# A fused spectral filter and feed-forward kernel: the column transforms halved by parity, the inverse in four PSUM banks, and part of LN2 moved into the first feed-forward block

## The chip, the cores and the metric

The kernel runs on one core of a Trainium2 chip. The metric is device time in microseconds (us). A profile's "span" runs from the first to the last instruction and is about 1.9 us shorter than the time. Each run also has a state; here "fast" runs have a granted TensorE clock of 0.99 or more. The engine names in the profile are PE (TensorE, matmul), PEld (its weight loads, which overlap matmuls), DVE (VectorE), ACT (ScalarE), POOL (GpSimd) and SP (SyncE, which issues DMAs). Matmuls write their results into PSUM banks; an "eviction" is the copy of such a result into SBUF, where the other operands lie. LN1 and LN2 are the two layer normalisations.

## The reference, cut to what matters

```python
x = A_x                                              # 1 x 2048 x 576, bf16
h = x + _A_ref(_layernorm(x), A_w_r, A_w_i)          # A: rfft2, times a complex filter, irfft2
h2 = h + _B_ref(_layernorm(h), w_gate, w_up, w_down) # B: (gelu(x @ w_gate) * (x @ w_up)) @ w_down, inner width 4608
```

The 2-D Fourier transform runs over 2048 positions and 576 channels (289 frequencies in the channel direction). The kernel does it with matmuls against tables of cosines and sines.

## The kernel before

The kernel has four stages, and inside the second and third each engine works through a fixed order of instructions.

1. **Start**: x is loaded, LN1 statistics are taken, and the position transform is begun.
2. **Filter loop**, 16 groups of frequencies. Per group: D (channel transform, matmuls), B (mixing, matmuls), an eviction Y, the complex product with the filter (T1, T2, then Z), and V (first step back, matmuls, then an eviction into SBUF). Within a turn of the loop the order is D of group i, B of group i-1, V of group i-3.
3. **Inverse**, 16 tiles: I (back to channels), an eviction G, N (back to positions), the residual add on VectorE, and the sum of squares for LN2. Four tiles are also normalised and transposed on TensorE for the first feed-forward block.
4. **FFN**: four blocks of gate and up matmuls (70 us) and down matmuls (35 us).

```python
    def st_D(i):                       # 2 x 5 matmuls of 289 columns
        ...
        for o in range(2):
            b = 2 * sl + o
            for dt in range(5):
                P.op(PE, ... t.matmul(bank(b, 0, 128, 0, K2), U[:, dt, g, :, :], FT[:, dt, o, 0:K2], start=(dt == 0), stop=(dt == 4)), ...)
            # o == 0: VectorE copies the bank to CUS; o == 1: ScalarE does

    def st_B(i):                       # 4 matmuls of 289 columns into banks 4 and 5, ScalarE evicts both to YS
        ...
        P.op(DVE, ... T1 = YS * WS ...)                              # 580 columns
        for pl in range(2):
            P.op(DVE, ... T2[pl] = YS[pl] * WS[1 - pl] ...)          # 290 columns each
        P.op(DVE, ... ZS[0] = T1[0] - T1[1] ...)
        P.op(DVE, ... ZS[1] = T2[0] + T2[1] ...)

    def st_V(i):                       # 4 matmuls of 256 columns to bank 6, 4 of 128 (half the array) to bank 7
        ...
        P.op(ACT, ... V[0:4] <- bank(6) ...)                         # 512 columns
        P.op(DVE, ... V[4] <- bank(7) ...)                           # 128 columns

    for i in range(NG + 3):
        if i < NG:
            st_D(i)
        if 1 <= i <= NG:
            st_B(i - 1)
        if i >= 3:
            st_V(i - 3)

    def st_I(c): ...                   # 2 x 5 matmuls of 288 columns, ScalarE evicts to GS
    def st_N(c): ...                   # 2 matmuls of 288 columns, VectorE adds to x (sum kept), ScalarE squares (sum kept)
```

(The cuts are marked with dots; comments are added.)

Of the kernel before, what the change touches and what calls it, by code (L numbers as in the profile page):

```python
# [11 lines left out]
ZW = 320  # L12
# [17 lines left out]
def build_tables():  # L30
# [28 lines left out]
    T["ITAB"] = I.reshape(128, 16 * 128)  # L59

    d = np.arange(D)[:, None]
    k2 = np.arange(K2)[None, :]
    ph = 2 * np.pi * ((d * k2) % D) / D
    fd = np.zeros((640, 2, KW))
    fd[:D, 0, :K2] = np.cos(ph)
    fd[:D, 1, :K2] = np.sin(ph)
    fd[:, 0, 0] = 0.0
    T["FTAB"] = fd.reshape(5, 128, 2 * KW).transpose(1, 0, 2).reshape(128, -1)

    B = np.zeros((2, 3, 16, 4, 2, 128))  # L70
# [40 lines left out]
    T["BTAB"] = B.reshape(2, 3, 128, 128).transpose(2, 0, 1, 3).reshape(128, -1)  # L111
# [3 lines left out]
    dc = np.arange(D)[None, :]  # L115
# [6 lines left out]
    dt_ = np.zeros((5, 128, D))  # L122
    dt_[0], dt_[1] = C[0:128], N[0:128]
    dt_[2], dt_[3] = C[128:256], N[128:256]
    dt_[4, 0:33] = C[256:289]
    dt_[4, 64:96] = N[256:288]
    T["EYE"] = np.eye(128)
    T["DTAB"] = dt_.transpose(1, 0, 2).reshape(128, -1)
# [156 lines left out]
def _build(nc, A_x, A_w_r, A_w_i, B_w_gate, B_w_up, B_w_down, out):  # L285
# [34 lines left out]
    FT = sb.alloc("FT", [128, 5, 2, KW], BF16)  # L320
    BT = sb.alloc("BT", [128, 2, 3, 128], BF16)
# [12 lines left out]
    V = sb.alloc("V", [128, 5, NT, NG, 8], BF16)  # L334
    DT = sb.alloc("DT", [128, 5, D], BF16)
    IT = sb.alloc("IT", [128, NT, 128], BF16)
    GS = sb.alloc("GS", [128, 2, D], BF16)
# [22 lines left out]
    P.op(POOL, lambda g: g.memset(WS[:, :, :, K2:KW], 0.0), w=["Wz"])  # L360
    P.op(POOL, lambda g: g.memset(U[64:128, 4, :, :, :], 0.0), w=["Uz"])
    xv = A_x[0].rearrange("(p c) d -> p c d", c=NT)
    ov = out[0].rearrange("(p c) d -> p c d", c=NT)
    for i, (c0, c1) in enumerate(((0, 2), (2, 4), (4, 8), (8, 12), (12, 16))):
        P.dma(SP, XO[:, c0:c1, :], xv[:, c0:c1, :], f"x{i}", w=[("X", c) for c in range(c0, c1)])
# [5 lines left out]
    def w_loads(pl, hf, eng):  # L371
        g0, g1 = ((1, 9), (9, 16))[hf]
        src = (A_w_r, A_w_i)[pl]
        o = []
        for jj in range(4):
            o.append((WS[jj:64:4, g0:g1, pl, 0:K2], (16 * jj + g0) * K2, [[128 * K2, 16], [K2, g1 - g0], [1, K2]], jj))
            o.append((WS[64 + jj:128:4, g0:g1, pl, 0:K2], (64 + 16 * jj + 16 - g0) * K2, [[128 * K2, 16], [-K2, g1 - g0], [1, K2]], 4 + jj))
        if hf:
            for p0 in range(2):
                o.append((WS[64 * p0:64 * p0 + 64, 0, pl, 0:K2], 64 * p0 * K2, [[128 * K2, 16], [16 * K2, 4], [1, K2]], 8 + p0))  # L380
        return [lambda d=d, off=off, ap=ap, h=h: P.dma(eng, d, bass.AP(src.tensor, off, ap), f"w{pl}{hf}", r=["Wz"], w=[("W", hf, pl, h)]) for d, off, ap, h in o]

    for f in w_loads(0, 0, SP) + w_loads(0, 1, SP):
        f()
# [3 lines left out]
    P.dma(SP, IT[:, :, :].rearrange("p a b -> p (a b)"), dram["ITAB"][:, :], "it", w=["IT"])  # L388
    P.dma(SP, IDT[:, :], dram["EYE"][:, :], "eye", w=["IDT"])

    P.op(POOL, lambda g: g.memset(YS[:, :, :, K2:KW], 0.0), w=["Yz"])
    P.op(POOL, lambda g: g.memset(ZS[:, :, :, K2:ZW], 0.0), w=["Zz"])
    for f in w_loads(1, 0, POOL):
        f()
    wrest = w_loads(1, 1, POOL)


    def ln1_act(q):
        c = 4 * q + 3
        P.op(ACT, lambda a, c=c: a.activation(JNK[:, 0, :], XO[:, c, :], ACTF.Identity, accum_out=SA[:, 0, c:c + 1]),  # L400
             r=[("X", c)], w=[("SA0", c), "J0"])
        P.op(ACT, lambda a, c=c: a.activation(JNK[:, 1, :], XO[:, c, :], ACTF.Square, accum_out=SA[:, 1, c:c + 1]),  # L402
             r=[("X", c)], w=[("SA1", c), "J1"])
# [5 lines left out]
    def ln1_var(q):  # L409
        for c in range(4 * q, 4 * q + 3):  # L410
            P.op(DVE, lambda v, c=c: v.bn_aggr(MV1[:, c, :], ST1[:, c, :, :]), r=[("ST1", c, 0), ("ST1", c, 1)], w=[("MV1", c)])
        c = 4 * q + 3
        P.op(DVE, lambda v, c=c: v.scalar_tensor_tensor(TM[:, 0, c:c + 1], SA[:, 0, c:c + 1], 1.0 / (D * D), SA[:, 0, c:c + 1],
                                                        op0=ALU.mult, op1=ALU.mult), r=[("SA0", c)], w=[("TM", c)])
        P.op(DVE, lambda v, c=c: v.scalar_tensor_tensor(MV1[:, c, 1:2], SA[:, 1, c:c + 1], 1.0 / D, TM[:, 0, c:c + 1],
                                                        op0=ALU.mult, op1=ALU.subtract), r=[("SA1", c), ("TM", c)], w=[("MV1", c)])

    def ln1_sqrt(q):
        cs = slice(4 * q, 4 * q + 4)
        P.op(ACT, lambda a, cs=cs: a.activation(RS1[:, cs], MV1[:, cs, 1], ACTF.Sqrt, bias=EPT[:, 0:1]),  # L420
             r=[("MV1", c) for c in range(4 * q, 4 * q + 4)] + ["EPT"], w=[("SD1", q)])

    def ln1_scale(q, eng):
        cs = slice(4 * q, 4 * q + 4)
        P.op(DVE, lambda v, cs=cs: v.reciprocal(RS1[:, cs], RS1[:, cs]), r=[("SD1", q)], w=[("RS1", q)])
        if eng == POOL:
            P.op(POOL, lambda g, cs=cs: g.tensor_tensor(ATS[:, cs, :], ATB[:, cs, :], RS1[:, cs].unsqueeze(2).to_broadcast([128, 4, 128]), op=ALU.mult),
                 r=[("RS1", q), "ATB"], w=[("ATS", c) for c in range(4 * q, 4 * q + 4)])
        else:
            for c in range(4 * q, 4 * q + 4):  # L430
                P.op(DVE, lambda v, c=c: v.tensor_scalar(ATS[:, c, :], ATB[:, c, :], RS1[:, c:c + 1], None, op0=ALU.mult),
                     r=[("RS1", q), "ATB"], w=[("ATS", c)])
# [5 lines left out]
    def a_mm(q, dt):  # L438
        b = (5 * q + dt) % 7
        w = 128 if dt < 4 else 64  # L440
        for i in range(4):
            c = 4 * q + i
            P.op(PE, lambda t, b=b, w=w, i=i, c=c, dt=dt: t.matmul(bank(b, 0, w, 128 * i, 128 * i + 128), XO[:, c, 128 * dt:128 * dt + w],
                                                                  ATS[:, c, :], start=True, stop=True),
                 r=[("X", c), ("ATS", c)], w=[("PS", b)])

    def a_ev(q, dt, eng):
        b = (5 * q + dt) % 7
        w = 128 if dt < 4 else 64
        src = bank(b, 0, w).rearrange("p (n g e) -> p n g e", n=4, g=16)  # L450
        dst = U[0:w, dt, :, 4 * q:4 * q + 4, :].rearrange("p g n e -> p n g e")
        if eng == DVE:
            P.op(DVE, lambda v, s=src, d=dst: v.tensor_copy(d, s), r=[("PS", b)], w=[("U", q, dt)])
        else:
            P.op(ACT, lambda a, s=src, d=dst: a.activation(d, s, ACTF.Copy), r=[("PS", b)], w=[("U", q, dt)])  # L455

    P.op(ACT, lambda a: a.activation(SA[:, 0, 0:1], EPT[:, 0:1], ACTF.Sqrt), r=["EPT"], w=[("SA0", 0)])
    ln1_act(0)
    ln1_act(1)
    idle_mm(24)  # L460
    for c in range(3):
        ln1_tile(c)
    ln1_var(0)
    ln1_sqrt(0)
    ln1_act(2)
    ln1_tile(4)
    ln1_scale(0, POOL)
    for f in wrest[:4]:
        f()
    ln1_tile(5)  # L470
    ln1_tile(6)
    ln1_var(1)
    a_mm(0, 0)
    a_ev(0, 0, ACT)
    ln1_sqrt(1)
    for dt in range(1, 5):
        a_mm(0, dt)
    a_ev(0, 1, ACT)
    a_ev(0, 2, ACT)
    ln1_tile(8)  # L480
    ln1_scale(1, POOL)
    for f in wrest[4:7]:
        f()
    ln1_tile(9)
    ln1_tile(10)
    ln1_var(2)
    a_ev(0, 3, ACT)
    a_ev(0, 4, ACT)
    ln1_sqrt(2)
    ln1_act(3)  # L490
    idle_mm(4)
    for dt in range(5):
        a_mm(1, dt)
        a_ev(1, dt, ACT)
    ln1_tile(12)
    ln1_scale(2, POOL)
    for f in wrest[7:]:
        f()
    ln1_tile(13)
    ln1_tile(14)  # L500
    ln1_var(3)
    ln1_sqrt(3)
    idle_mm(4)
    for dt in range(5):
        a_mm(2, dt)
    a_ev(2, 0, ACT)
    a_ev(2, 1, DVE)
    ln1_scale(3, DVE)
    a_ev(2, 2, ACT)
    a_ev(2, 3, DVE)  # L510
    a_ev(2, 4, ACT)
    idle_mm(4)
    for dt in range(5):
        a_mm(3, dt)
        a_ev(3, dt, (ACT, DVE)[dt % 2])
    idle_mm(3)


    ukeys = [("U", q, dt) for q in range(4) for dt in range(5)] + ["Uz"]

    def st_D(i):
        g = GORD[i]
        sl = i % 2
        for o in range(2):
            b = 2 * sl + o
            for dt in range(5):
                P.op(PE, lambda t, b=b, o=o, dt=dt, g=g: t.matmul(bank(b, 0, 128, 0, K2), U[:, dt, g, :, :], FT[:, dt, o, 0:K2],  # L527
                                                                 start=(dt == 0), stop=(dt == 4)),
                     r=ukeys + ["FT"], w=[("PS", b)])
            if o == 0:  # L530
                P.op(DVE, lambda v, b=b, sl=sl: v.tensor_copy(CUS[:, sl, 0, 0:K2], bank(b, 0, 128, 0, K2)), r=[("PS", b)], w=[("CU", sl)])
            else:
                P.op(ACT, lambda a, b=b, sl=sl: a.activation(CUS[:, sl, 1, 0:K2], bank(b, 0, 128, 0, K2), ACTF.Copy), r=[("PS", b)], w=[("SU", sl)])  # L533

    def st_B(i):
# [3 lines left out]
        for b, tabs in ((4, (0, 1)), (5, (1, 2))):  # L539
            for o in range(2):  # L540
# [238 lines left out]
```

## Time and profile before

The time before is 518.28 us (median of 4 runs; 518.22 to 519.13). TensorE is busy for almost the whole span; the first lines of the profile's page are:

```profile
span 516.4 us, 10131 instructions
## 1 busy us (share of the span) xinstructions
PE 507.4 (98%) x4425; PEld 295.9 (57%) x4427; DVE 184.5 (36%) x428; ACT 152.7 (30%) x285; POOL 27.8 (5%) x48
```

The chain of waits, in order of time, has these columns: start (us), duration (us), engine and what it did. This is one full turn of the filter loop and one tile of the inverse, in the kernel before:

```profile
29.36 1.34 PE PS L527 x10
30.70 0.50 PE PS L541 x4
31.20 0.44 PE PS L560 x4
31.64 0.24 PE PS L564 x4
31.87 1.34 PE PS L527 x10
...
67.02 1.23 PE PS L602 x10
68.25 0.24 PE PS L611 x2
68.49 1.23 PE PS L602 x10
```

L527 is D, L541 is B, L560 and L564 are V, L602 is I and L611 is N. Everything on the chain is TensorE, so the loop has a period of 31.87 - 29.36 = 2.51 us and the inverse one of 1.47 us, both TensorE's. This is VectorE's own timeline. Each line has start, duration, engine, line, operation, and in brackets the idle time before it and what ended it:

```profile
34.44 0.46 DVE L546 TENSOR_TENSOR T_79<-YS,WS 128x580 bf16<-128x580 bf16 x1 [0.60 <-ACT YS L544]
34.81 0.52 DVE L548 TENSOR_TENSOR T_80<-YS,WS 128x290 bf16<-128x290 bf16 x2
35.25 0.30 DVE L550 TENSOR_TENSOR ZS<-T_79 128x290 bf16<-128x290 bf16 x1
...
35.89 0.45 DVE L531 CAST CUS<-PS 128x289 bf16<-128x289 f32 x1
36.95 0.46 DVE L546 TENSOR_TENSOR T_79<-YS,WS 128x580 bf16<-128x580 bf16 x1 [0.60 <-ACT YS L544]
```

### The profile page before, as it was taken

Reading aid. Unit: us, or ns where it says so; the run is one execution under the profiler, and the core shown is the slowest. Engines: PE = TensorE matmul, PEld = TensorE weight load, DVE = VectorE, ACT = ScalarE, POOL = GpSimd, SP = SyncE. Lnnn points to the kernel's source line nnn. Section 1 sums busy time; section 2 is a strip of 40 time slices with the busy share of each in tenths; the row PEclk is TensorE's granted clock in tenths of the full one; section 3 lists DMA queues with packets and bytes.
Section 4 is the critical chain, followed back from the end, with each engine's and each line's share of the span. In section 5 each row is a group of like instructions: output and inputs, shape, how many; then the busy total and the mean of one; then the engine's idle time right before and its main releaser. Section 6 shows DMA issues by size and latency. Waiting matters only on the chain.

```text
span 516.4 us, 10131 instructions
## 1 busy us (share of the span) xinstructions
PE 507.4 (98%) x4425; PEld 295.9 (57%) x4427; DVE 184.5 (36%) x428; ACT 152.7 (30%) x285; POOL 27.8 (5%) x48
## 2 busy tenths in 40 slices
PE   8899899999999999999999999999999999999997
PEld 3577577444445775444457754444477644444776
DVE  5687758344432112443321124433311133333111
ACT  5756677423521002332320013323200033233000
POOL 8800130000000000000000000000000000000000
PEclk9999999999999999999999999999999999999999
DMA  8999791011000000110000000100000000000000
GB/s 289 289 343 307 208 361 44 4 24 22 7 1 2 18 18 11 22 22 11 1 1 18 18 11 20 22 15 1 1 13 18 18 1 1 0 2 1 13 18 17
DMA packets 23899, 28.64 MB, mean 55 GB/s; under 512 B 11408, under 2 KB 17680, under 8 KB 23856
## 3 DMA queue, kind: packets, MB, share of 16 engines
q1 hardware_dynamic: 20560, 15.68, 10.9%
q0 software_dynamic: 3152, 11.80, 7.0%
q8 instruction: 34, 0.56, 0.5%
q10 hardware_dynamic: 144, 0.52, 0.3%
q14 instruction: 9, 0.07, 0.0%
HBM read 23.67 MB, written 2.36 MB: 50 GB/s over the span
## 4 chain that ended last, share of the span: by engine, by line
PE 93%; DVE 2%; ACT 2%; DMA 2%; issue 0%; SPq 0%; DVEq 0%
PE PS L699 55%; PE PS L720 27%; PE PS L527 4%; PE PS L602 3%; DMA XO<-in_A_x_dram 2%; PE PS L541 1%; ACT U L455 1%; PE PS L560 1%; PE PS L611 1%; PE PS L564 1%; DVE XO L614 0%; ACT JNK L400 0%; DVE ST_53 L407 0%; ACT JNK L402 0%; ACT YS L544 0%
## 5 line engine op out<-in xcount | busy, mean ns | idle before, releaser
L711 ACT ACTIVATE GL<-PS 128x512 bf16<-128x512 f32 x144 | 85.8, 597 | 293.9 <-PE PS L699 293.1
L712 DVE TENSOR_TENSOR AT<-GL,PS 128x512 bf16<-128x512 bf16 x144 | 98.9, 688 | 174.3 <-PE PS L699 169.8
L699 PE MATMUL PS<-HT_69,WGU 64*128 64x512 bf16 x1296 | 144.4, 376 | 0.0
L699 PE MATMUL PS<-HT_84,WGU 64*128 64x512 bf16 x1296 | 144.4, 376 | 0.0
L720 PE MATMUL PS<-WD,AT 128*128 128x288 bf16 x1152 | 141.8, 286 | 0.0
L720 PEld LDWEIGHTS PS<-WD,AT 128*128 128x128 bf16 x1152 | 112.4, 98 | 29.9 <-issue 1.7
L699 PEld LDWEIGHTS PS<-HT_84,WGU 64*128 64x128 bf16 x1296 | 64.5, 94 | 77.9 <-issue 0.5
L699 PEld LDWEIGHTS PS<-HT_69,WGU 64*128 64x128 bf16 x1296 | 64.5, 94 | 76.8 <-issue 0.7
L723 DVE TENSOR_TENSOR OS<-PS,XO 128x288 bf16<-128x288 f32 x32 | 14.6, 458 | 126.0 <-PE PS L720 126.0
L602 PE MATMUL PS<-DT,V 128*128 128x288 bf16 x160 | 22.1, 286 | 0.5 <-ACT V L567 0.5
L527 PE MATMUL PS<-FT,U 128*128 128x289 bf16 x160 | 22.3, 287 | 0.2 <-ACT U L455 0.2
L602 PEld LDWEIGHTS PS<-DT,V 128*128 128x128 bf16 x160 | 15.4, 98 | 4.3 <-issue 0.6
L527 PEld LDWEIGHTS PS<-FT,U 128*128 128x128 bf16 x160 | 14.5, 97 | 5.1 <-issue 0.4
L614 DVE SCALAR_TENSOR_TENSOR XO<-PS,XO 128x576 bf16<-128x576 f32 x16 | 12.1, 756 | 9.6 <-PE PS L611 9.3
L436 PE MATMUL PS<-ZD 128*128 128x512 bf16 x37 | 11.8, 475 | 1.5 <-POOL ZD L358 1.3
L617 ACT ACTIVATE SQ<-XO 128x576 bf16<-128x576 bf16 x16 | 10.9, 682 | 5.0 <-DVE XO L614 4.8
L407 DVE BATCH_NORM_STATS2 ST_53<-XO 128x6 f32<-128x288 bf16 x24 | 9.2, 443 | 5.7 <-DMA XO<-in_A_x_dram 5.7
L544 ACT ACTIVATE YS<-PS 128x578 bf16<-128x578 f32 x16 | 10.5, 655 | 1.8 <-PE PS L541 0.7
L604 ACT ACTIVATE GS<-PS 128x576 bf16<-128x576 f32 x16 | 10.2, 635 | 2.6 <-PE PS L602 2.6
L541 PE MATMUL PS<-CUS,BT 128*128 128x289 bf16 x64 | 10.6, 286 | 0.2
L533 ACT ACTIVATE CUS<-PS 128x289 bf16<-128x289 f32 x16 | 6.6, 413 | 14.0 <-PE PS L527 14.0
L546 DVE TENSOR_TENSOR T_79<-YS,WS 128x580 bf16<-128x580 bf16 x16 | 7.3, 459 | 9.1 <-ACT YS L544 9.1
(57 smaller groups left out, 173.2 us busy)
## 6 DMA issues: line engine op xcount, KB each, us to landing
WD<-in_B_w_down_dram POOLq DMA_DIRECT2D x9, 576.0 KB, 9.3
WGU<-in_B_w_gate_dram POOLq DMA_DIRECT2D x4, 1152.0 KB, 17.7
WGU<-in_B_w_up_dram SPq DMA_DIRECT2D x4, 1152.0 KB, 22.5
out_dram<-OS SPq DMA_DIRECT2D x32, 72.0 KB, 1.6
XO<-in_A_x_dram SPq DMA_DIRECT2D x3, 576.0 KB, 8.2
FT<-c_ftab SPq DMA_DIRECT2D x1, 725.0 KB, 12.7
DT<-c_dtab SPq DMA_DIRECT2D x1, 720.0 KB, 14.6
HT_84<-HN SPq DMA_TRANSPOSE x40, 2.4
```

Source lines behind the costliest of these rows:

```text
L436: P.op(PE, lambda t: t.matmul(bank(7), ZD[:, 0:128], ZD[:, :], start=True, stop=True), r=["ZD"], w=[("PS", 7)])
L527: P.op(PE, lambda t, b=b, o=o, dt=dt, g=g: t.matmul(bank(b, 0, 128, 0, K2), U[:, dt, g, :, :], FT[:, dt, o, 0:K2], start=(dt == 0), stop=( ...
L541: P.op(PE, lambda t, b=b, o=o, tb=tabs[o], sl=sl, sp_=sp_: t.matmul(bank(b, 0, 128, 0, K2), BT[:, sp_, tb, :], CUS[:, sl, o, 0:K2], start= ...
L544: P.op(ACT, lambda a, sl=sl: a.activation(YS[:, sl, :, 0:K2], banks(4, 2, K2), ACTF.Copy), r=[("PS", 4), ("PS", 5)], w=[("Y", sl)])
L602: P.op(PE, lambda t, b=b, h=h, kt=kt, c=c: t.matmul(bank(b, 0, 128, 0, 288), V[:, kt, c, :, :], DT[:, kt, 288 * h:288 * h + 288], start=(k ...
L614: P.op(DVE, lambda v, x2=x2, c=c: v.scalar_tensor_tensor(x2, banks(4, 2, 288), 1.0, x2, op0=ALU.mult, op1=ALU.add, accum_out=SB2[:, 0, c:c ...
L617: P.op(ACT, lambda a, sl=sl, c=c: a.activation(SQ[:, sl, :], XO[:, c, :], ACTF.Square, accum_out=SB2[:, 1, c:c + 1]), r=[("X", c)], w=[("S ...
L699: op = P.op(PE, lambda t, h0=h0, kt=kt, wt=wt, f=f, b=b, HT=HT, s=(half == 0 and j in (0, 5)), e=(half == 1 and j in (3, 8)): t.matmul(ban ...
L711: P.op(ACT, lambda a, s2=s2, b0=b0: a.activation(GL[:, s2, :], bank(b0), ACTF.Gelu_apprx_tanh), r=[("PS", b0)], w=[("GL", s2)])
L712: P.op(DVE, lambda v, s2=s2, b0=b0, f=f: v.tensor_tensor(AT[:, f, :], GL[:, s2, :], bank(b0 + 1), op=ALU.mult), r=[("GL", s2), ("PS", b0 + ...
L720: P.op(PE, lambda t, b=b, h=h, f=f, p=p: t.matmul(bank(b, 0, 128, 0, 288), AT[:, f, 128 * p:128 * p + 128], WD[:, f, 288 * h:288 * h + 288 ...
L723: P.op(DVE, lambda v, b=b, h=h, p=p, c=c: v.tensor_tensor(OS[:, p % 2, 288 * h:288 * h + 288], bank(b, 0, 128, 0, 288), XO[:, c, 288 * h:2 ...
```

## The change

The intent is to cut TensorE's work in the filter loop and the inverse.

- Cosines and sines of frequency k and 288 - k differ only by a sign that depends on the parity of the channel d. So D computes the even and the odd channels separately for half of the frequencies (2 x 3 matmuls of 290 columns), and VectorE makes both halves by adding and subtracting. B takes one of its operands in two halves with opposite signs.
- V does its tail in full-array matmuls (6 of 256 columns), and one ScalarE eviction of 768 columns takes the whole result. T2 becomes one operation, and the subtract and add that make Z go to GpSimd (for all but the last two groups).
- The inverse uses the same parity: I has 6 matmuls, N has 4 and reads one half backwards; N alternates between two pairs of PSUM banks.
- The squares of tiles 4 to 15 and their LN2 statistics move into FFN block one. The start uses six groups of tiles in place of four. All filter weights load from SyncE's queue, and GpSimd issues the gate weights after its last Z.

```diff
     def st_D(i):
-            for dt in range(5):
-                ... t.matmul(bank(b, 0, 128, 0, K2), U[:, dt, g, :, :], FT[:, dt, o, 0:K2], start=(dt == 0), stop=(dt == 4))
+            for dt in range(3):
+                us = (2 * o + dt) if dt < 2 else 4
+                ... t.matmul(bank(b, 0, 128, 0, 2 * HK), U[:, us, g, :, :], FT[:, o, dt, :], start=(dt == 0), stop=(dt == 2))
-        # one bank copied by VectorE, one by ScalarE
+        P.op(ACT, ... a.activation(ES[:, sl, :], bank(2 * sl, 0, 128, 0, 2 * HK), ACTF.Copy), ...)
+        P.op(DVE, ... v.tensor_tensor(CUS[:, sl, :, 0:HK], e2, o2, op=ALU.add), ...)
+        P.op(DVE, ... v.tensor_tensor(CUS[:, sl, :, K2 - 1:HK - 1:-1], e2[:, :, 0:HK - 1], o2[:, :, 0:HK - 1], op=ALU.subtract), ...)
     def st_B(i):
-        for b, tabs in ((4, (0, 1)), (5, (1, 2))):         # 4 matmuls of 289
+        for b, tabs in ((4, (0, 1, 3)), (5, (1, 2, 0))):   # 2 of 289, 4 of 145 or 144
...
+        P.op(DVE, ... v.tensor_tensor(T2[:, sl, :, :], YS[:, sl, :, :], WS[:, g, 1::-1, :], op=ALU.mult), ...)
+        z3 = i % 3
+        ze = POOL if i < NG - 2 else DVE
+        P.op(ze, ... ZS[:, z3, 0, 0:KW] = T1[0] - T1[1] ...)
+        P.op(ze, ... ZS[:, z3, 1, 0:KW] = T2[0] + T2[1] ...)
     def st_V(i):
+        for c in range(3):
+            b, o = 6 + c // 2, 256 * (c % 2)                # every group in banks 6 and 7
...
+        P.op(ACT, ... V[:, :, :, g, :] <- PS[:, 6 * 512:6 * 512 + 768] ...)
     for i in range(NG + 3):
+        if i > NG:
+            idle_ft(5, 2 * (i - NG - 1))                    # filler matmuls
...
     def st_N(c):
-            b = 4 + h
+            b = 4 + 2 * sl + h
+            for i in range(2):
+                rhs = GS[:, sl, i, 288:0:-1] if h else GS[:, sl, i, 0:288]
...
+        if c < 4:
+            square(c, SQ[:, sl, :], ("SQ", sl))
...
+            if tb == 0 and f < 12:
+                square(4 + f, OS[:, f % 2, :], ("OS", f % 2, 0))   # inside FFN block one
```

(The tables, the loads, the grouping of the start and the LN2 bookkeeping are left out, and so is the eviction of the transposes, which moves from VectorE to ScalarE. The fillers are matmuls whose results nobody reads.)

## The prediction

> **What bounds it now.** TensorE is busy 98% of the 516.4 us span, and 93% of the chain of waits. In time order the chain has four stages. (1) Start, 0 to 21.8 us: LN1 and column transform; ScalarE (sums, PSUM evictions) is the last link. (2) Filter loop, 21.8 to 58.8 us: a steady 2.51 us per group, TensorE gapless, then a tail to 64.2. (3) Inverse, 64.2 to 89.6 us: 1.47 us per tile on TensorE, plus four transposes (0.44 us each) and 0.5 us of waits. (4) FFN to the end, whose matmuls the change leaves alone.
>
> **The change, in durations from the trace.** A matmul of 288 columns takes 0.1225 us in the chain, of 256 columns 0.109, of 128 columns 0.0625.
> - Filter loop, per group: row transform 10 matmuls (1.24 us) to 6 (0.74). Mixing step 4 full to 2 full and 4 half ones: 0.50 as before. Its tail from 4 x 256 columns and 4 half-array matmuls with a bubble (0.77) to 6 x 256 (0.65). TensorE: 2.51 to 1.89 us.
> - Inverse, per tile: 10 to 6 matmuls (-0.49), but 2 to 4 in the last step (+0.245): 1.47 to 1.225 us.
> - Added: an fp32 ScalarE copy (0.41) and two VectorE combines (cadence 0.39) for the two old evictions; a V eviction of 768 columns (estimate 0.82, from 0.59 at 512 and 0.655 at 578). The filter product's subtract/add go to GpSimd: 0.6 to 0.7 each, estimated from 1.05 us for 512 columns there. Per group: ScalarE 1.65, VectorE 1.55, GpSimd 1.3 us, all under 1.89.
> - LN2 squares of tiles 4 to 15 (0.87 us each) move into FFN block one, where ScalarE uses 0.6 of 1.95 us per step: free. The built program has no more activation-table loads.
> - All filter weights load from SyncE (36 issues of 0.81 us), landing by about 37 us; needed near 39. GpSimd issues the gate weights only near 50 us; needed near 78.
>
> **Contention.** The Trainium skill, "GPSIMD Engine Reference", Key points, says GpSimd shares SBUF interfaces with VectorE, with contention against VectorE instructions with two SBUF inputs. The two filter products are such (0.37 each). The trace of before does not show the size. 1.3 + 0.74 would exceed 1.89 if they exclude each other; I allow 0.05 to 0.1 us per group.
>
> **Sum.** Start 0 (six smaller groups start sooner, but ten more evictions). Filter loop 16 x 0.62 = -9.9, +0.8 slower fill, +1.0 contention. Tail -0.6. Inverse 15.5 x 0.245 = -3.8, +0.2 waits. FFN 0. Total about -12.3 us, all on the chain: predicted **506.0 us**, 8 in 10 range **502.0 to 510.0**. Chances: faster by over 2% (under 507.9) 0.74, within 2% 0.25, slower 0.01.
>
> **What would show it.** Right: loop period 1.9 to 2.0 us, TensorE near-gapless; inverse period 1.22; FFN begins at 76 to 79 us and lasts 427 as before; GpSimd products under 0.8 us. Wrong: TensorE waiting on GpSimd, or its products over 0.9 us; VectorE waiting for weights at the ninth group; TensorE waiting on the 768-column eviction (single buffered); first FFN steps waiting on gate weights; the start ending after 22.5 us.
>
> **What would make it wrong.** Reversed or stride-2 operands below full rate on TensorE; half-width matmuls bound by weight loads; GpSimd and VectorE excluding each other (loop at 2.1 us: 509 us); late weights; or, the other way, a start that ends 1 to 2 us earlier.

## The result, and the profile after

The time after is 511.47 us (median of 4 runs, 511.30 to 511.59) against 518.28 us (518.22 to 519.13) for the kernel before. The ratio is 0.9865, 95% interval 0.9848 to 0.9882. Ratios here are the mean time of one kernel's fast runs over that of the other's in the same rounds, so they are not quite the ratio of the medians. The gain is 1.35%. By the medians it is 6.8 us where about 12.3 were forecast, and the time lies outside the range of 502 to 510.

```profile
span 509.6 us, 10004 instructions
...
PE 497.7 (98%) x4337; PEld 289.6 (57%) x4337; DVE 183.1 (36%) x375; ACT 158.6 (31%) x296; POOL 42.1 (8%) x60
```

The page looks the same, at 98% of TensorE. The stages have to be set side by side. The table is made from TensorE's timeline of both profiles: the first D matmul, the fifth and the sixteenth D, the third-last V, the first I, and the first FFN matmul.

| Stage, us | before | after | difference | predicted |
|---|---|---|---|---|
| Start, to the first D | 21.80 | 22.05 | +0.25 | 0 |
| Loop fill: first to fifth D | 7.50 | 6.83 | -0.67 | |
| Loop middle: 11 periods | 27.61 | 21.69 | -5.92 | |
| Loop end: 16th D to third-last V | 3.16 | 3.32 | +0.16 | |
| (fill, middle and end together) | 38.27 | 31.84 | -6.43 | -8.1 |
| Tail: third-last V to first I | 4.09 | 5.27 | +1.18 | -0.6 |
| Inverse | 25.40 | 23.30 | -2.10 | -3.6 |
| FFN | 426.84 | 427.14 | +0.30 | 0 |
| Span | 516.40 | 509.60 | -6.80 | -12.3 |

The middle of the loop did what was forecast (2.51 to 1.97 us per group). The missing 5.5 us lie in the rest of the loop (1.7), the tail (1.8), the inverse (1.5) and small terms in the start and the FFN (0.55).

**VectorE in the loop.** Here are VectorE's and GpSimd's lines of the timeline after, a little over one period:

```profile
44.01 0.70 POOL L567 TENSOR_TENSOR ZS<-T_80 128x290 bf16<-128x290 bf16 x1
44.10 0.45 DVE L547 TENSOR_TENSOR CUS<-ES,PS 128x290 bf16<-128x290 f32 x1
44.47 0.45 DVE L548 TENSOR_TENSOR CUS<-ES,PS 128x288 bf16<-128x288 f32 x1
44.83 0.45 DVE L563 TENSOR_TENSOR T_80<-YS,WS 128x580 bf16<-128x580 bf16 x1
44.85 0.96 POOL L568 TENSOR_TENSOR ZS<-T_81 128x290 bf16<-128x290 bf16 x1
45.20 0.92 DVE L564 TENSOR_TENSOR T_81<-YS,WS 128x580 bf16<-128x580 bf16 x1
46.05 0.45 DVE L547 TENSOR_TENSOR CUS<-ES,PS 128x290 bf16<-128x290 f32 x1
```

VectorE has no idle time. The second filter product, L564, has the same shape as the first, L563 (0.45 us), but takes 0.92 us: it ends 0.31 us after the GpSimd add that it overlaps has ended (45.81 to 46.12), as if it had only then begun to move data. (In some groups it is the first product that is long, as with 0.98 us at 50.76.) GpSimd's add, in turn, takes 0.96 us where the subtract beside the combines takes 0.70. VectorE's loop is 1.95 us, when the sum without the lengthening would be about 1.5. The waits view of VectorE says the same in total. Its columns are who waited, for whom, us in total, times, longest. First the kernel before (22 to 60 us):

```profile
DVE T_79 L546 <- ACT YS L544: 9.1, 13, 1.9
DVE CUS L531 <- PE PS L527: 1.8, 2, 1.0
```

and the kernel after, in the same stretch:

```profile
DVE CUS L547 <- ACT ES L544: 1.2, 1, 1.2
DVE T_80 L563 <- ACT YS L561: 0.9, 1, 0.9
```

VectorE went from 10.9 us of waiting to two waits (2.1 us), both in the fill. TensorE's work per group fell from 2.51 to about 1.91 us, and VectorE's went from 1.91 to 1.95.

**The tail.** This is the chain of waits after, from the last product on:

```profile
53.89 0.83 PE PS L577 x6
...
54.74 0.82 ACT V L580
...
55.61 0.84 PE PS L577 x6
...
56.48 0.82 ACT V L580
...
59.16 1.66 PE PS L627 x12
```

V matmuls and their eviction take turns, because every group uses banks 6 and 7 (the lines left out are issue times and the last such pair): 1.73 us per group.

**The inverse.** Its chain shows two loops through other engines. First the early tiles, then the tiles with a transpose (L689):

```profile
60.91 0.67 PE PS L642 x4
...
61.60 0.78 DVE XO L645 x2
...
62.40 0.78 ACT SQ L633 x2
63.17 0.55 ACT GS L629
...
63.77 0.68 PE PS L642 x4
...
71.46 0.51 PE PS L642 x4
...
71.99 0.77 DVE XO L645 x2
72.76 0.57 DVE HN L671 x2
...
73.37 0.45 PE PS L689 x5
...
74.57 0.51 PE PS L642 x4
```

From one N to the N of two tiles later the first loop takes 63.77 - 60.91 = 2.86 us, where TensorE's own work for two tiles is 2.48 (it runs 1.24 per tile wherever nothing interferes). The second takes 3.11 us, against about 2.92 of work with the transpose.

### The profile page after: what moved, and what is told of

It is laid out like the page before. It is cut to its first block, busy times and chain, and to the rows that moved or that the text cites. A ratio compares the mean times of both kernels' runs of the same rounds, so it can differ in the third digit from the quotient of the medians.

```text
span 509.6 us, 10004 instructions
## 1 busy us (share of the span) xinstructions
PE 497.7 (98%) x4337; PEld 289.6 (57%) x4337; DVE 183.1 (36%) x375; ACT 158.6 (31%) x296; POOL 42.1 (8%) x60
## 4 chain that ended last, share of the span: by engine, by line
PE 90%; DVE 4%; ACT 3%; DMA 1%; POOL 1%; issue 1%; SPq 0%; DVEq 0%; POOLq 0%
PE PS L731 55%; PE PS L752 28%; PE PS L577 2%; PE PS L541 2%; DMA XO<-in_A_x_dram 1%; PE PS L642 1%; PE PS L558 1%; PE PS L627 1%; DVE XO L645 1%; DVE U L474 1%; ACT U L476 1%; ACT V L580 0%; ACT JNK L411 0%; POOL ZS L568 0%; PE PS L689 0%
## 5 line engine op out<-in xcount | busy, mean ns | idle before, releaser
L627 PE MATMUL PS<-DT,V 128*128 128x289 bf16 x96 | 14.4, 287 | 0.4 <-ACT V L580 0.4
L541 PE MATMUL PS<-FT,U 128*128 128x290 bf16 x96 | 14.4, 287 | 0.3 <-DVE U L474 0.3
L577 PE MATMUL PS<-VT,ZS 128*128 128x256 bf16 x96 | 13.1, 272 | 1.0 <-ACT V L580 0.6
L580 ACT ACTIVATE V<-PS 128x768 bf16<-128x768 f32 x16 | 13.0, 810 | 3.3 <-PE PS L577 2.8
L568 POOL TENSOR_TENSOR ZS<-T_81 128x290 bf16<-128x290 bf16 x14 | 12.3, 878 | 2.4 <-DVE CUS L548 0.5
L564 DVE TENSOR_TENSOR T_81<-YS,WS 128x580 bf16<-128x580 bf16 x16 | 12.5, 778 | 0.0
L558 PE MATMUL PS<-CUS,BT 128*128 128x289 bf16 (+2 forms) x96 | 10.7, 246 | 1.1 <-DVE CUS L548 0.8
L629 ACT ACTIVATE GS<-PS 128x578 bf16<-128x578 f32 x16 | 10.3, 647 | 3.7 <-PE PS L627 3.4
L642 PE MATMUL PS<-GS,IT 128*128 128x288 bf16 x64 | 10.5, 286 | 0.8 <-ACT GS L629 0.7
L452 PE MATMUL PS<-ZD 128*128 128x512 bf16 x30 | 10.0, 485 | 1.3 <-POOL ZD L370 1.3
```

Source lines behind the costliest of these rows:

```text
L541: P.op(PE, lambda t, b=b, o=o, dt=dt, us=us, g=g: t.matmul(bank(b, 0, 128, 0, 2 * HK), U[:, us, g, :, :], FT[:, o, dt, :], start=(dt == 0) ...
L558: P.op(PE, lambda t, b=b, tb=tb, pl=pl, q0=q0, q1=q1, m=m, sl=sl, sp_=sp_: t.matmul(bank(b, 0, 128, q0, q1), BT[:, sp_, tb, :], CUS[:, sl, ...
L577: P.op(PE, lambda t, b=b, o=o, c=c, zp=zp, sl=sl, sp_=sp_: t.matmul(bank(b, 0, 128, o, o + 256), ZS[:, sl, zp, 128 * c:128 * c + 128], VT[ ...
L580: P.op(ACT, lambda a, g=g: a.activation(V[:, :, :, g, :], PS[:, 6 * 512:6 * 512 + 768].rearrange("p (k n e) -> p k n e", k=6, n=16), ACTF. ...
L627: P.op(PE, lambda t, b=b, h=h, i=i, kt=kt, c=c: t.matmul(bank(b, 0, 128, 0, K2), V[:, kt, c, :, :], DT[:, 3 * h + i, 0:K2], start=(i == 0) ...
L642: P.op(PE, lambda t, b=b, h=h, i=i, c=c, rhs=rhs: t.matmul(bank(b, 0, 128, 0, 288), IT[:, h * i, c, :], rhs, start=(i == 0), stop=(i == 1) ...
```

## The experiments

Sixteen kernels were run. Unless told otherwise each is the kernel after with one edit. "Loop and tail" runs from the first D to the first I: 42.36 us before, 37.11 after. The start code is the same in all of them but three (e7, e17 and e15), yet the start in their profiles ends anywhere from 21.52 to 22.05 us; so a time can move by half a microsecond for that alone, and the stage lengths decide.

### e1: the whole product on VectorE

```diff
-        ze = POOL if i < NG - 2 else DVE
+        ze = DVE
```

> The changed kernel with the filter product's subtract and add on VectorE for all 16 groups (GpSimd does none of them). Theory (GpSimd and VectorE exclude each other: in the trace of after, the second product takes 0.92 us when a GpSimd operation runs beside it and 0.46 when none does, so VectorE is full at the loop's 1.95 us): the second product falls back to 0.46 us in every group, and VectorE has 4 x 0.37 + 2 x 0.22 = 1.92 us per group, so the loop's period stays within 0.06 us of 1.95; the first V step no longer waits for GpSimd, which is worth up to 0.9 us in the fill and 0.2 us before the tail; time 510.2 to 511.7. Rival (the lengthening is only how the profiler shows it, and VectorE has slack): the period rises to 1.92 + 0.45 = 2.3 us or more, and the time to over 514.

Measured: 511.85 us, ratio 0.9869 (0.9841 to 0.9898); loop and tail 38.47 us. The second product fell back to 0.46 us, as expected, and in the undisturbed part the period was 1.91 us. But a new wait appeared at the ninth group:

```profile
DVE T L563 <- DMA WS<-in_A_w_i_dram: 2.0, 1, 2.0
```

With no Z on GpSimd, its queue issued the gate weights from 18.2 us on instead of 53.7 us, and they crowded the filter weights: the last of these (63 KB each, from A_w_i) took 14.5 us from issue to landing in place of 2.4 (medians). So GpSimd's Z steps also have a good effect: they hold the gate loads back, as the prediction had noted ("only near 50 us"). The fill (first D to first V) stayed at 6.2 us, so the expectation that GpSimd costs up to 0.9 us in the fill was wrong.

### e5: the same, with the gate load held

```diff
+        # first gate load also depends on the V of group 9
+        r=([("V", 9)] if o == 0 and j == 0 else [])
```

> As e1_z_on_vector, and the first gate load waits until group 9 has left the loop, so that it can't crowd the filter weights as it did there (VectorE waited 1.98 us for them at the ninth group). Theory (GpSimd's share of the product costs the loop[...]): no wait for weights; the period is 1.91 us as in the undisturbed part of e1, against 1.97 of after; filter loop and tail together 36.4 to 36.8 us against 37.11; time 510.0 to 510.9. The fill (first row-transform matmul to first V matmul) stays at 6.2 us, since it did in e1. Rival (VectorE as the only one loses more in the tail): loop and tail 37.0 us or more.

Measured: 510.51 us, ratio 0.9837 (0.9821 to 0.9852); loop and tail 36.39 us. The period is 1.91 us, the weight wait is gone, and the fill is unchanged at 6.25. Taking the work back from GpSimd gains 0.7 us once the gate loads are held. The move of Z to GpSimd was therefore a small loss in itself.

### e2 and e9: the tail

e2 gives the last two V groups banks 0-1 and 2-3, which are free by then; e9 also drops the fillers between them.

```diff
-            b, o = 6 + c // 2, 256 * (c % 2)
+            b0 = {NG - 2: 0, NG - 1: 2}.get(i, 6)
+            b, o = b0 + c // 2, 256 * (c % 2)
...                                     # eviction from bank b0 too
-        if i > NG:                      # e9 only; in e2 the fillers go to bank 4
-            idle_ft(5, 2 * (i - NG - 1))
```

> The changed kernel with the V matmuls of the last two groups in four PSUM banks that are free by then, the fillers in another. Theory (the tail is the chain V matmuls 0.83, eviction 0.81, V matmuls of the next group, because all V groups share one pair of banks): the three V groups no longer wait for each other's eviction, three evictions of 0.81 us run back to back, or the last V waits for its filter product at about 1.8 us after the first; the tail from the first of the last three V groups to the first inverse matmul falls from 5.27 to 3.5 to 4.1 us, time 509.9 to 510.5. Rival (late filter products pace the tail): no change beyond 0.3 us.

> As e2_tail_banks, without the two rows of fillers between the last V groups. Theory (in e2 the fillers, 0.61 us each in TensorE's order, delayed V matmuls that were ready): the tail from the first of the last three V groups to the first inverse matmul falls from e2's 4.35 to about 3.7 us, loop and tail from 36.21 to about 35.6, time 509.4 to 510.0. Rival (the fillers keep TensorE's clock up and pay): the granted clock falls below 0.99 in the inverse and it lengthens by more than 0.3 us.

Measured: e2 510.26 us, ratio 0.9837 (0.9811 to 0.9863), tail 5.27 to 4.35 us, less gain in the tail than expected (3.5 to 4.1): the V matmuls now stood behind fillers of 0.61 us each. e9 509.61 us, ratio 0.9821 (0.9802 to 0.9839), tail 3.67 us, loop and tail 35.54, as expected, and the clock in the inverse stayed at 1.00. So the shared banks and the fillers together cost 1.6 us in the tail; the late-product rival is out for this part.

### e3: the squares one tile later

```diff
-        if c < 4:
-            square(c, SQ[:, sl, :], ("SQ", sl))
+        if 1 <= c < 5:
+            square(c - 1, SQ[:, 1 - sl, :], ("SQ", 1 - sl))
```

> The changed kernel with the ScalarE squares of tiles 0 to 3 queued one tile later, so that the eviction of the inverse's tile c+1 stands before the square of tile c-1. Theory (in the first five tiles the square waits at the head of ScalarE's queue for the VectorE residual add, and the eviction that the next matmuls need stands behind it: 2.87 us for two tiles against 2.48 of TensorE work): two tiles take 2.5 to 2.6 us there, the inverse shortens by 0.6 to 1.3 us, time 510.2 to 510.9. Rival (TensorE itself is slower there, by the reversed reads or the four matmuls): no change.

Measured: 510.33 us, ratio 0.9838 (0.9807 to 0.9869); the inverse shortened from 23.30 to 22.52 us, and the early tiles ran at 1.24 us each. The square at the head of ScalarE's queue was waiting for the residual add while the eviction behind it was ready. TensorE's reversed reads are not slow: with this wait gone, I and N together take 1.24 us for ten matmuls, two of which read backwards.

### e4: normalisation ahead of the residual add

```diff
         st_I(c)
+        if c in (8, 10, 12):
+            norm((c - 6) // 2)
         if c >= 1:
             st_N(c - 1)
-        if c in (6, 8, 10, 12):
-            norm((c - 6) // 2)
+        if c == 6:
+            norm(0)
```

> The changed kernel with the normalisation of tiles 1 to 3 queued on VectorE before the residual add of the same step instead of after it. Theory (the transposes wait for the normalisation, which stands behind a residual add that itself waits for matmuls: 3.11 us for two tiles and a transpose against 2.92 of TensorE work): the three waits of TensorE on the normalisation, 0.17 us each, go; the inverse shortens by 0.4 to 0.7 us, time 510.8 to 511.1. Rival: the waits move to the residual add, no change.

Measured: 510.67 us, ratio 0.9844 (0.9818 to 0.9870); the three waits of TensorE on the normalisation are gone and the inverse is 22.71 us, -0.59. (The time is a little under the expected 510.8; its start ended at 21.63.)

### e7: what makes VectorE wait for GpSimd

In the start after, a one-element VectorE operation (L430) took 0.98 us while GpSimd scaled a table:

```profile
15.78 1.04 POOL L442 TENSOR_TENSOR ATS<-ATB,RS_56 128x512 bf16<-128x512 bf16 x1 [1.81 <-DVE RS_56 L440]
15.85 0.98 DVE L430 SCALAR_TENSOR_TENSOR MV_54<-SA,TM 128x1 f32<-128x1 f32 x1
```

GpSimd's operation beside it (L442) ran from 15.78 to 16.82. e7 rewrites the eight operations L424 and L430 so that they have one tensor input and a scalar pointer.

```diff
-  v.scalar_tensor_tensor(MV1[:, c, 1:2], SA[:, 1, c:c + 1], 1.0 / D, TM[:, 0, c:c + 1], ...)
+  v.tensor_scalar(MV1[:, c, 1:2], SA[:, 1, c:c + 1], 1.0 / D, TM[:, 0, c:c + 1], ...)
```

> The changed kernel with the eight 1-element VectorE operations of LN1 that have two SBUF tensor inputs rewritten to one tensor input and a scalar pointer. Theory (what makes VectorE wait for GpSimd is the second SBUF read): the operation that took 0.98 us beside a 1.04 us GpSimd product in the start (0.16 elsewhere) takes 0.2 us or less, the start ends 0 to 0.5 us sooner. Rival (any VectorE operation with an SBUF input waits): still near 1 us.

Measured (one run, 510.92 us, state unknown as for any single run). The same place in e7, again beside a GpSimd operation (15.53 to 16.57):

```profile
15.53 1.04 POOL L442 TENSOR_TENSOR ATS<-ATB,RS 128x512 bf16<-128x512 bf16 x1 [1.82 <-DVE RS L440]
15.67 0.21 DVE L430 TENSOR_SCALAR MV<-SA,TM 128x1 f32<-128x1 f32 x1
```

0.98 became 0.21 us. A second such meeting in the start agrees: 0.54 us at 8.35, up to the end of a GpSimd operation (8.87), became 0.21 us. The edit changes the instruction together with the number of its inputs; but the combines (L547, L548), which are the same instruction as the products (TENSOR_TENSOR) with one input in PSUM, keep 0.45 us beside GpSimd. So it is the second SBUF tensor input that waits for GpSimd, and it waits until GpSimd's operation is over.

### e18: GpSimd only beside one-input steps

VectorE does T1, the subtract, T2; GpSimd does the add alone, which then falls beside the two combines (one SBUF input and one PSUM input).

```diff
         P.op(DVE, ... T1 = YS * WS ...)
+        z3 = i % 3
+        P.op(DVE, ... ZS[:, z3, 0, 0:KW] = T1[0] - T1[1] ...)
         P.op(DVE, ... T2 = YS * WS reversed ...)
-        P.op(ze, ... ZS[:, z3, 0, 0:KW] = T1[0] - T1[1] ...)
         P.op(ze, ... ZS[:, z3, 1, 0:KW] = T2[0] + T2[1] ...)
```

> The changed kernel with that re-ordering alone. Theory: period 1.91 to 1.93 us in place of 1.97, TensorE's waits at the end of the loop shorter; loop and tail 36.1 to 36.6 us against 37.11, time 510.3 to 510.9. Rival: no change beyond 0.2 us.

Measured: 510.23 us, ratio 0.9837 (0.9820 to 0.9855); loop and tail 36.10 us, 1.01 less than after; period 1.91. The timeline shows why:

```profile
36.95 0.46 DVE L566 TENSOR_TENSOR T<-YS,WS 128x580 bf16<-128x580 bf16 x1
37.34 0.46 DVE L547 TENSOR_TENSOR CUS<-ES,PS 128x290 bf16<-128x290 f32 x1
37.48 0.67 POOL L569 TENSOR_TENSOR ZS<-T 128x290 bf16<-128x290 bf16 x1 [1.24 <-DVE T L566]
37.71 0.45 DVE L548 TENSOR_TENSOR CUS<-ES,PS 128x288 bf16<-128x288 f32 x1
```

The second product (L566) is 0.46 us again, GpSimd's add 0.67 us, and the combines beside it keep their 0.45. Where nothing else holds VectorE, in the fill, its loop is now 1.82 us (combine at 26.21, the next at 28.03), under TensorE's 1.91. That VectorE's work in the kernel before was also 1.91 us is chance.

### e10 and e13: V one group later

A longer lead was tried against the fill: four product buffers, and V of group i-4 in place of i-3. e13 adds it to e11 below.

```diff
-    ZS = sb.alloc("ZS", [128, 3, 2, ZW], BF16)
+    ZS = sb.alloc("ZS", [128, 4, 2, ZW], BF16)
-        if i >= 3:
-            st_V(i - 3)
+        if i >= 4:
+            st_V(i - 4)
```

> The changed kernel with V one group later in the loop (four product buffers in place of three; the squares write another scratch buffer for room). Theory (the fill is not short of work but of time: each new group must pass ScalarE's copy, two VectorE combines, the mixing, an eviction, two products and the GpSimd step before its V, and TensorE waits for that in its fixed order): the fifth row-transform starts before the first V, TensorE's wait for the first V's product (0.23 us and more) goes, and the fill is worth 0.3 to 0.8 us; part is given back in the tail, where four V groups stand in a row at 1.73 us each; net between -0.6 and +1.2 us, with the first D matmul to the fifth at 6.1 to 6.5 us against 6.83. Rival (the fill waits only for VectorE's queue): the fifth row transform starts no earlier.

> e11_all_vector and V one group later in the loop, as in e10, whose profile fell in a slow state. If the fill is a matter of latency: the fifth row transform starts 6.0 to 6.4 us after the first, in place of 6.8, and loop and tail fall by 0.2 to 0.6 us against e11, since the tail no longer costs 1.73 us per V group; time 506.8 to 507.7. If VectorE's queue sets the fill: no change against e11, or a loss of up to 0.5 us by the longer tail.

Measured: e10 512.36 us (median of its three fast runs), ratio 0.9872 (0.9853 to 0.9891); its profiled run fell in a slow state (653.2 us at a clock of 0.752), so its trace is not used. e13 508.62 us, ratio 0.9815 (0.9802 to 0.9828). In e13 the fifth D does start earlier (6.21 us after the first), but the next B then waits 0.50 us for VectorE's combine, and the sixteenth D comes 27.92 us after the first, as in e11 (27.93). (The first V stands a turn later by design.) Loop and tail are 36.03 us, 0.89 longer than e11: missed, mainly because with four groups in the tail two of them share a pair of banks again (a wait of 0.90 us). A longer lead does not mend the fill.

### e11, e12 and e14: the mends together

e11 joins e9, e3, e4 and e5; e12 joins e9, e3 and e4 and leaves Z on GpSimd as in the change; e14 is the kernel after, unaltered, on the same chip.

> Four mends at once: the last V groups in free PSUM banks without fillers between, the squares one tile later, the normalisations ahead of the residual add, and the whole filter product on VectorE with the first gate load held until group 9. If the losses found one by one are separate and add: loop and tail 34.7 to 35.2 us (37.11 in after), inverse 21.7 to 22.2 us (23.30), start and FFN as in after, time 507.2 to 508.0, which is 3.5 to 4.3 us under after. If the mends share a cause or the waits only move: less than 2.5 us under after.

> The first three mends of e11_all_vector, with the filter product's last step left on GpSimd as in the change. If the GpSimd step costs the loop about 0.05 us per group and 0.2 us before the tail also when the tail is mended: loop and tail 35.4 to 35.7 us, time 507.8 to 508.6, 0.4 to 0.8 us over e11.

> The changed kernel unaltered, on the chip of the three combined kernels, so that they can be set against it there: 511.0 to 512.0 us, ratio to before 0.985 to 0.988; the start ends between 21.5 and 22.1 us, the spread over the runs so far; the other stages within 0.1 us of the first trace.

Measured: e11 507.95 us, ratio 0.9801 (0.9787 to 0.9814); e12 508.10 us, ratio 0.9804 (0.9791 to 0.9818); e14 511.25 us, ratio 0.9866 (0.9853 to 0.9880). In both the inverse is 21.92 to 21.93 us, so the savings of e3 and e4 add (0.78 + 0.59 = 1.37; measured 1.37 to 1.38). Loop and tail are 35.14 us (e11) and 35.51 us (e12). The times of the two differ less than expected (0.15 us); e12's start ended 0.30 us earlier, which hides most of the 0.37 us between their loops. All stages of e14 are within 0.1 us of the first trace, the start (21.96 against 22.05) included.

### e15 and e16: is VectorE the pace?

Both edit e11. e15 cuts the subtract to 2 columns (wrong results; a memset in the start also grows, so that all of ZS is zero); e16 does it twice.

```diff
-  ... ZS[:, z3, 0, 0:KW] = T1[0] - T1[1]                # e11
+  ... ZS[:, z3, 0, 0:2] = T1[0, 0:2] - T1[1, 0:2]       # e15
+  ... ZS[:, z3, 0, 0:KW] = T1[0] - T1[1]   (twice)      # e16
```

> e11_all_vector with the subtract of the filter product cut to 2 columns in every group (wrong results on purpose): VectorE loses 0.1 to 0.15 us of its 1.92 per group. Theory (VectorE sets fill and end of the loop, TensorE its middle): the period stays 1.91, TensorE's wait before the last mixing step (0.59 us) and before the last V (0.74) shrink or go; loop and tail 34.2 to 34.7 us against 35.14. Rival (latency alone, VectorE has slack): 35.0 to 35.2.

> e11_all_vector with the subtract done twice in every group (correct results, 0.22 us of VectorE more per group). Theory (VectorE has no slack in the loop): the period rises to 2.13 us and loop and tail to 38.2 to 38.8 us, +3.1 to +3.6; time 510.8 to 511.7. Rival (VectorE has 0.35 us of slack per group, as the prediction had it): under 35.8 us.

Measured: e15 507.38 us (results wrong), loop and tail 34.61, -0.53 against e11, as expected; the period stayed at 1.91. Of the 0.53, only 0.09 lie in the fill (first to fifth D), 0.19 between the sixteenth D and the third-last V, and 0.25 in the tail. (The cut shortens the chain to Z as well as VectorE's work, so it does not tell the two apart.) e16 513.02 us, ratio 0.9891 (0.9874 to 0.9908), loop and tail 40.33, +5.19, more than expected. The size was off because the extra step costs 0.35 us of VectorE (35.06 to 35.41), not 0.22; that the second write waits for the first is the likely reason, not tested. With that, VectorE's six kinds of steps, one after the other without idle time, take 2.26 us from one combine to the same combine of the next group (33.59 to 35.85; L567 and L568 are the doubled subtract):

```profile
33.59 0.45 DVE L547 TENSOR_TENSOR CUS<-ES,PS 128x290 bf16<-128x290 f32 x1
...
35.06 0.31 DVE L567 TENSOR_TENSOR ZS<-T 128x290 bf16<-128x290 bf16 x1
35.41 0.31 DVE L568 TENSOR_TENSOR ZS<-T 128x290 bf16<-128x290 bf16 x1
35.63 0.30 DVE L569 TENSOR_TENSOR ZS<-T 128x290 bf16<-128x290 bf16 x1
35.85 0.45 DVE L547 TENSOR_TENSOR CUS<-ES,PS 128x290 bf16<-128x290 f32 x1
```

The period of TensorE's V steps became just that, 2.26 us. In e11, with the whole product on VectorE, VectorE has no slack: add 0.35 us to it and the loop slows by 0.35. The rival named above is out for e11. But this is not the prediction's slack: that was 1.89 - 1.55 = 0.34 us with Z on GpSimd. What shows that the change itself had none is its own trace above, where VectorE never idles in the loop (1.95 us).

### e17: the fastest

e17 is e12 with the one-input form of e7 and the order of e18.

> The three mends of e12_all_gpsimd, the one-input form of e7, and the filter product re-ordered: VectorE does product, subtract, product, GpSimd only the add, which then falls beside the two combines (one SBUF input and PSUM) instead of beside the products. Theory (exclusion only against steps with two SBUF inputs): VectorE 1.70 us per group, no product of 0.92 us in the loop, the period TensorE's 1.91; loop and tail 34.5 to 35.0 us; time 506.9 to 507.8, the fastest. Rival (GpSimd's add still meets the products): 35.3 us or more.

Measured: 507.42 us, ratio 0.9783 (0.9766 to 0.9799), all correct; loop and tail 34.94, inverse 21.91. It beats the kernel before by 2.2% and the kernel after by 3.8 us (against e14's 511.25, measured on another chip beside the same kernel before). TensorE's remaining waits in the loop are 0.40 and 0.70 us for combines in the fill, 0.24 before the last B, and 0.74 us for the last product.

## Why the prediction was right or wrong

Three terms of the sum failed: the tail (-0.6 forecast, +1.18 measured), the waits of the inverse (+0.2 forecast, about +1.7 measured), and the loop outside its middle, together with VectorE's slack (1.7 us short).

**Right.** TensorE's work fell as forecast: 2.51 to about 1.91 us per group (e1, e5, e18 run at it) and 1.47 to 1.24 us per tile (e3). The period of the loop, 1.97 us, lay in "1.9 to 2.0 us". The 768-column eviction took 0.81 us (estimate 0.82). The Trainium skill, "ScalarE: Activation LUTs", What ACT_TABLE_LOAD costs, gives 186 ns + 0.833 ns per column for such an operation (with immediate scale and bias), an estimate of 0.826 us: the trace agrees. The squares inside FFN block one were free: the FFN is 0.30 us longer, and the last N step, which runs inside it in both kernels, alone has two more matmuls (0.25 us). The start gave nothing, as said. The filter weights came in time in the change itself.

**Wrong: "Per group: ScalarE 1.65, VectorE 1.55, GpSimd 1.3 us, all under 1.89."** VectorE takes 1.95. The prediction did name the risk that GpSimd and VectorE exclude each other, and allowed "0.05 to 0.1 us per group" for it. That is right for the period (1.97 against 1.89), but the size was a guess, as it said itself, so the fit is in part luck. (For full exclusion it expected a loop at 2.1 us; the exclusion is there, but only one of GpSimd's two steps falls beside a product, the other beside the combines.) It treated the wait as a small addition to TensorE's pace, when it takes all of VectorE's slack. What that costs is seen in e18: without it the middle of the loop is 0.64 us shorter, the loop's end 0.34 (3.32 to 2.98) and the fill 0.04. The page that decides this was not used: the Trainium skill, "SBUF — State Buffer", SBUF: two separate sides, says that the pair of ports the two engines share is "an exclusive lock, not a bandwidth split", held for the whole instruction. The traces agree: 0.98 us for a one-element operation beside a GpSimd operation of 1.04 us, 0.21 us with one tensor input (e7), 0.92 against 0.46 us for the product (e18). It also stood in the trace before that VectorE worked 1.91 of 2.51 us per group. A loop cannot go below 1.91 us if VectorE's work stays there; the forecast of 1.55 rested on moving Z away, and the wait (0.46 us) took back what the move had saved (e5, with Z on VectorE, runs at 1.91).

**Wrong: "+0.8 slower fill", and no loss at the loop's end.** The three parts of the loop gave 6.4 us where 8.1 were forecast. Of the 1.7 us between them, 0.36 is arithmetic: V's saving of 0.12 us was counted for 16 groups, and three of the V lie in the tail. By TensorE's own work (0.50 us less per D, 0.12 per V) the fill should have gained 2.12 us, the middle 6.82 and the end 0.62. They lost 1.45, 0.90 and 0.78 of that; 0.8 was allowed for the fill, 1.0 for contention and nothing for the end. So the middle is covered, and the fill and the end are not. At the end VectorE answers for about 0.3 us (e18). In the fill it is not shown to: with less on VectorE the fill shortened by no more than 0.09 us (e15; 0.04 in e18), more on it lengthened it by 0.36 (e16), and more lead (e13) did not help. How much of the fill is VectorE's queue and how much the bare length of the chain D, copy, combine, B, eviction, product, Z is not settled.

**Wrong in sign: "Tail -0.6".** It came out at +1.18 us. The prediction listed the single-buffered eviction among the things that could go wrong, but did not follow it through: with nothing else left to do, the V groups cost matmul plus eviction, 1.73 us each. e9 gets 1.6 us back. It also measured the old tail from another mark (58.8 us, the end of the last but one B; the third-last V starts at 60.07), so that the tail of before looked like 5.4 us instead of 4.1.

**Wrong: "Inverse 15.5 x 0.245 = -3.8, +0.2 waits".** The saving of TensorE's work was right, the waits were not +0.2 but about 1.7 us. When TensorE's tile went from 1.47 to 1.24 us, two loops became the longer ones: N, residual add, square, eviction, N (2.86 us per two tiles; it would have fitted into the old 2.94), and N, residual add, normalisation, transpose (3.11). e3 and e4 change only the order of two instructions and give back 0.78 and 0.59 us; about 0.3 of the 1.7 stays unexplained.

The summary of the sums: the forecast of -12.3 us missed 5.5. The mends that only undo the waits (e9, e3, e4 and the VectorE order of e18, together in e17 with e7) take the time to 507.42 us, 11 us under the kernel before. What is left against the forecast lies almost all in the loop and its tail: 34.94 us in e17, where the forecast came to 33.7 (42.36 - 8.7).

## What to carry to other kernels

Before cutting the work of the bounding engine, write down the per-period work of every other engine from its timeline, waits taken out: the second-longest sum, here 1.91 us of VectorE beside 2.51 of TensorE, is the floor of the new period unless the change takes work off that engine, and work moved to GpSimd is only off VectorE if VectorE's neighbouring steps do not have two SBUF inputs. Then walk the loops that pass through several engines (matmul, add, square, eviction, matmul) and ask whether they still fit into the shorter period; often the mend is only an order in a queue. Finally, give the last turns of a loop their own sum: there is no other work to hide a matmul and its eviction from each other, so they want separate buffers and no fillers in front.

## What the Trainium skill lacked or had wrong

- "GPSIMD Engine Reference", Key points, speaks of contention with VectorE instructions with two SBUF inputs but not of its size. The runs show a full wait: 0.98 us instead of 0.16 for a one-element operation beside a GpSimd operation of 1.04 us. ("SBUF — State Buffer" has it right; the first page would have been enough with one sentence of it.)
- "GPSIMD Engine Reference", Elementwise — side-by-side cycle accounting, gives about 2.6 cycles per element for a two-input operation, and no time for GpSimd's dispatch. At the page's 1.2 GHz this is an estimate of 1.11 us for 512 columns without any dispatch; the table scaling in the start (a product, one input broadcast) took 1.04 us in all. With 0.61 us for 256 columns there, the runs give 1.67 ns per column, an estimate of 2.0 cycles, and about 0.18 us besides; the add of 290 columns fits (0.67 us when nothing held it, e18). These are bf16; the page's figures are fp32.
- "TensorE: Matmul & The Clock Gate", Back-to-back issue gap, gives about 81 ns for sustained 128-column matmuls with their weight loads. Here 20 of them (4 with 64 weight columns) took 1.41 us from the first start to the last end (e7, at 13.76 us); less the last one's 0.22 us that is 62.6 ns from start to start, and the measurement decides.
- No run here contradicts "SBUF — State Buffer" or "ScalarE: Activation LUTs" where they were used.
